# Reading v in long runs, streaming heads in blocks of 64 queries, and half an expert's weights moved

## Chip, cores and metric

One core of one Trainium2 chip. The metric is the device time of one execution in microseconds (us). Most executions agree within 1%; some fall into a slower state (over 1.5% above the fastest of the same kernel), and only fast executions are compared here. A ratio is the mean time of one kernel's fast runs over the mean of the fast runs of the kernel before in the same rounds, on the same chip, so it is not quite the ratio of the medians that I quote. Profiled spans are about 1.5 us shorter than the time of the same execution, and one execution of each kernel was profiled, which need not be its median.

## The reference

Causal attention over 4 batches of 8 heads with 768 positions of 64 numbers. Three heads are retrieval heads (they see everything before), five are streaming heads (they see the first 4 positions, the sinks, and the last 64). The result, 3072 rows of 512, goes through a top-1 mixture of 8 experts with a skip gate.

```python
stream_keep = causal & (is_sink | in_win)          # n_sink 4, window 64
mask = where(is_retrieval, causal, stream_keep)    # heads 1 0 1 0 0 0 1 0
a = softmax(where(mask, scale * q @ k.T, -1e9))
x = (a @ v).transpose(0, 2, 1, 3).reshape(3072, 512)
do = (x @ w_skip) > 0
e = argmax(x @ w_gate)                             # for rows with do
x[do] += softmax(x @ w_gate)[e] * (relu(x @ w1[e]) @ w2[e])
```

## The kernel before

Attention walks over 16 pairs of heads. In each batch three pairs are mixed (retrieval and streaming), one has two streaming heads. In turn i the engines score pair i, transpose q and k of pair i+1, weigh v of pair i-1 and feed the routing of pair i-2. PE, DVE and GpSimd run in the written order.

```python
vv = v.rearrange("b h (n p) d -> b p h n d", p=P)      # 256-byte runs

def cast_v(i):                                          # GpSimd
    va, vx = vab[i % 2], vxb[i % 2]
    nc.gpsimd.tensor_copy(va[:, :, :, :D], v32[i])
    if i:
        nc.scalar.activation(xgs[i], xgs[0], ACT.Copy)
    for hi, hh in enumerate(heads(i)[1]):
        if not IS_RETR[hh]:                             # rows for the window + sinks
            nc.gpsimd.tensor_copy(vx[:, hi], va[:, hi, :NQB - 1])
            nc.gpsimd.tensor_copy(vx[:N_SINK, hi], ...)

# score(i, hi, c0): a streaming head has 11 blocks of 128x128 columns, scored and
# exponentiated in two pieces, 1024 and 384 wide                        (cut)
# weigh(i, hi): streaming heads add va and vx, block by block           (cut)

        ins = nc.gpsimd.tensor_copy(x16s[i], xh[:, :, h2:h2 + 2])
        if i in (0, 5, 10, 11, 12, 13):                 # six halves of weights
            load_weight()
# ... and one more half behind the last gate transpose                  (cut)

for i in range(NPR + 2):
    cast_v(i); load_qk(i + 3); load_v(i + 2)            # bounds cut
    step(0); transpose(i + 1, "q"); step(1); weigh(i - 1, 0)
    step(2); transpose(i + 1, "k"); cast_qk(i + 2)
    # routing of an earlier batch, step(3), gate transpose              (cut)
    weigh(i - 1, 1); step(4)
    # more routing, gate_logits                                         (cut)

gather(0, 4); load_weight(1); gather(4, 6); load_weight(1)
gather(6, 8); load_weight(); rows(0); first(0); rows(1)  # experts follow
```

The softmax here doesn't subtract the row's maximum and nothing guards it: scores larger than these inputs give would overflow.

Of the kernel before, what the change touches and what calls it, by code (L numbers as in the profile page):

```python
# [18 lines left out]
B = 4  # L19
# [240 lines left out]
def kernel(  # L260
# [100 lines left out]
    for e in range(E // 2):  # L361
        for half in range(2):
            wtile(e, half, wpool)
    wtile(E // 2, 0, wpool)
    xgs = [const.tile([P, DM], FP32, name=f"xg{t}") for t in range(NT)]
# [28 lines left out]
    kv = k.rearrange("b h (p n) d -> b p h (n d)", p=P)  # L394
    vv = v.rearrange("b h (n p) d -> b p h n d", p=P)
    Ov = out.rearrange("(b n p) d -> b p n d", b=B, p=P)
# [9 lines left out]
    RLEN = pos  # L406
    SLEN = (2 * NQB - 1) * P
    CH = 1024

    with tc.tile_pool(name="ac", bufs=1) as ac_pool, \  # L410
# [4 lines left out]
         tc.tile_pool(name="st_ps", bufs=2, space=bass.MemoryType.PSUM) as st_psum, \  # L415
         tc.tile_pool(name="tr_ps", bufs=2, space=bass.MemoryType.PSUM) as tr_psum, \
         tc.tile_pool(name="at", bufs=2) as at_pool, \
         tc.tile_pool(name="ov_ps", bufs=2, space=bass.MemoryType.PSUM) as ov_psum, \
         tc.tile_pool(name="oo", bufs=3) as o_pool, \
# [18 lines left out]
        nc.vector.memset(xgs[0], 0.0)  # L438

        NPR = B * H // 2  # L440
        qk32, v32, qk16, qT, ats, xhs, x16s, xTs = ({} for _ in range(8))
        gpss = {}

        def make_masks():





            def select(m, base, column, row):  # L450
                nc.gpsimd.affine_select(
                    out=m, in_=m, compare_op=ALU.is_ge, fill=-MASKED,
                    base=base, pattern=[[column, P]], channel_multiplier=row)

            rmask = ac_pool.tile([P, P], FP16, name="rmask")
            nc.gpsimd.memset(rmask, 0.0)
            select(rmask, 0, 1, -1)
            band = ac_pool.tile([P, P], FP16, name="band")
            nc.gpsimd.memset(band, 0.0)
            select(band, 0, 1, -1)  # L460
            select(band, WINDOW - 1, -1, 1)
            saux = ac_pool.tile([P, P], FP16, name="saux")
            nc.gpsimd.memset(saux, 0.0)
            select(saux, WINDOW - 1 - P, -1, 1)
            nc.gpsimd.memset(saux[:N_SINK], 0.0)
            smask = ac_pool.tile([P, 2 * NQB - 1, P], FP16, name="smask")
            nc.vector.tensor_copy(
                smask[:, :NQB], band.unsqueeze(1).to_broadcast([P, NQB, P]))
            nc.vector.tensor_copy(smask[:N_SINK, 0], rmask[:N_SINK])
            nc.vector.tensor_copy(  # L470
                smask[:, NQB:], saux.unsqueeze(1).to_broadcast([P, NQB - 1, P]))
            return smask.rearrange("p n c -> p (n c)"), rmask

# [14 lines left out]
        def load_v(i):  # L488
            b, hs = heads(i)
            vf = ld_pool.tile([P, 2, NQB, D], FP32, tag="vf", name="vf")  # L490
            for hi, hh in enumerate(hs):
                nc.sync.dma_start(out=vf[:, hi], in_=vv[b, :, hh])
            v32[i] = vf
# [8 lines left out]

        def cast_v(i):
            va, vx = vab[i % 2], vxb[i % 2]
            nc.gpsimd.tensor_copy(va[:, :, :, :D], v32[i])  # L505
            if i:
                nc.scalar.activation(xgs[i], xgs[0], ACT.Copy)  # L507
            for hi, hh in enumerate(heads(i)[1]):
                if not IS_RETR[hh]:
                    nc.gpsimd.tensor_copy(vx[:, hi], va[:, hi, :NQB - 1])  # L510
                    nc.gpsimd.tensor_copy(
                        vx[:N_SINK, hi], va[:N_SINK, hi, 0:1].to_broadcast(
                            [N_SINK, NQB - 1, D + 1]))

# [23 lines left out]

        def pieces(retr):


            work = [(i * P, i, i, 1) for i in range(NQB)]
            if retr:
                for j in range(NQB - 1):
                    work.append((RCOL[j, j + 1], j, j + 1, NQB - 1 - j))
            else:
                for i in range(1, NQB):
                    work.append(((NQB - 1 + i) * P, i - 1, i, 1))
            cut = []
            for (c, j, i, n) in work:  # L550
                while n:
                    m = min(n, 4 - (c // P) % 4)
                    cut.append((c, j, i, m))
                    c, i, n = c + m * P, i + m, n - m
            return cut
# [13 lines left out]
        def score(i, hi, c0):  # L569
            retr = IS_RETR[heads(i)[1][hi]]  # L570
            cn = min(CH, (RLEN if retr else SLEN) - c0)
            pst = st_psum.tile([P, CH], FP32, tag="pst", name="pst")
            mn = S if retr else SLEN
            work = [w for w in pieces(retr) if c0 <= w[0] < c0 + CH]
            for bank in range(c0, c0 + cn, 512):
                mw = min(mn - bank, 512)
                if mw > 0:
                    nc.tensor.matmul(  # L578
                        pst[:, bank - c0:bank - c0 + mw], C.ident,
                        rmask.unsqueeze(1).to_broadcast([P, mw // P, P])  # L580
                        if retr else smask[:, bank:bank + mw],
                        start=True, stop=False)
                here = [w for w in work if bank <= w[0] < bank + 512]
                for (c, j, qb, n) in here:
                    last = (c, j, qb, n) == here[-1]
                    kz, cols = kzb[i % 2][:, hi], slice(c - c0, c - c0 + n * P)
                    if retr or j == qb:
                        nc.tensor.matmul(  # L588
                            pst[:, cols], kz[:, j * P:(j + 1) * P],
                            qT[i][:, qb * P:(qb + n) * P], start=mw <= 0,  # L590
                            stop=mw <= 0 or last)
                        continue


                    nc.tensor.matmul(  # L595
                        pst[WINDOW:, cols], kz[:, j * P + WINDOW:(j + 1) * P],
                        qT[i][:, qb * P:(qb + 1) * P], start=False, stop=last)
                    if last:
                        n0 = sum(w[1] != w[2] for w in here)
                        nc.tensor.matmul(  # L600
                            pst[:WINDOW, c - c0 - (n0 - 1) * P:c - c0 + P],
                            kz[:, :WINDOW],
                            qT[i][:, (qb + 1 - n0) * P:(qb + 1) * P],
                            start=False, stop=True)
            b0 = base(i, hi) + c0
            nc.scalar.activation(ats[i][:, b0:b0 + cn], pst[:, :cn], ACT.Exp,  # L606
                                 scale=SCALE)

        def weigh(i, hi):
# [6 lines left out]
            else:  # L616
                plan = []
                for qb in range(NQB):
                    plan.append((qb, qb * P, va[:, hi, qb]))
                    if qb:  # L620
                        plan.append((qb, (NQB - 1 + qb) * P,
                                     vx[:, hi, qb - 1]))
            opsa = ov_psum.tile([P, NQB, D + 1], FP32, tag="opsa",
                                name="opsa")
            for n, (qb, c, vb) in enumerate(plan):
                nc.tensor.matmul(  # L626
                    opsa[:, qb, :], ats[i][:, b0 + c:b0 + c + P], vb,
                    start=(n == 0), stop=(n == len(plan) - 1))
            if i % 2 == 0 and hi == 0:
# [18 lines left out]
            if not last:  # L648
                ins = nc.gpsimd.tensor_copy(x16s[i], xh[:, :, h2:h2 + 2])  # L649
                if i in (0, 5, 10, 11, 12, 13):  # L650
                    with tc.issue_after(ins.ins):
                        load_weight()
# [11 lines left out]
        def gate_transpose(i):  # L664
# [18 lines left out]
            if i == NPR - 1:  # L683

                nc.gpsimd.tensor_copy(mark, xTg[:, 0, :1])
                load_weight()

        def gate_logits(i):
# [139 lines left out]
        with tc.manual_schedule(engines=engines):  # L828
# [10 lines left out]
            transpose(0, "k")  # L839
            cast_qk(1)  # L840
            for i in range(NPR + 2):
                cur = chunks(i) if i < NPR else []
# [38 lines left out]
                if i > 5 and b < B - 1 and late == 2:  # L881
                    right(b)
                if i >= 2:
                    gate_logits(i - 2)
# [3 lines left out]
            cnt = sums[:, 512:512 + E]  # L888
            idle = st_psum.tile([P, CH], FP32, tag="pst", name="idle")[:, :512]
            place(B - 1)  # L890
            left(B - 1)
# [21 lines left out]
    with tc.tile_pool(name="moe_w", bufs=1) as mw_pool, \  # L913
# [5 lines left out]

        for e in range(E // 2, E):  # L920
            for half in range(2):
# [91 lines left out]
        with tc.manual_schedule(engines={mybir.EngineType.Pool,  # L1013
                                         mybir.EngineType.PE,
                                         mybir.EngineType.DVE}):
            gather(0, 4)
            load_weight(1)
# [64 lines left out]
```

## Time and profile before

| what | where it is read | value |
|---|---|---|
| time | median of 3 executions | 204.39 us |
| span profiled | page | 201.9 us |
| second qT copy (end of the start) | timeline of ACT | 12.5 us |
| second to last qT copy (the loop) | timeline of ACT | 87.3 us |
| last qT copy to first gather (the tail) | timelines of ACT and GpSimd | 27.3 us |
| first gather to the first row cast | timelines of GpSimd and DVE | 3.3 us |
| first gather to the end (routing done, experts) | as above | 74.8 us |

In the profiles PE is TensorE, ACT ScalarE, DVE VectorE and POOL GpSimd; pst are scores in PSUM, at their exponentials, va is v in float16, vx its shifted copy, opsa the weighted sums, xh these sums divided, and qT and kz the transposed q and k. R1 and R2 in the prediction are the two pieces in which a retrieval head is scored.

ACT copies qT out of PSUM exactly once per pair, so these copies are the clock of the loop: their distances are the lengths of the turns.

### The profile page before, as it was taken

How to read it: one execution, taken by the hardware profiler on the slowest of the kernel's cores; microseconds unless marked ns; L12 is line 12 of the kernel's file. 1: busy time of each engine (PE TensorE's matmuls, PEld its weight loads, DVE VectorE, ACT ScalarE, POOL GpSimd, SP SyncE). 2: the span in 40 equal slices, each digit the busy share in tenths (PEclk: the TensorE clock that was granted, in tenths of full speed). 3: DMA queues.
4: the chain of work that ended last, by engine and by line, in shares of the span. 5: the costliest groups of instructions: out<-in, count | busy, mean ns of one | idle time of the engine just before them, and what ended most of it. 6: DMA issues, size and time to landing. Idle time of an engine off the chain costs nothing.

```text
span 201.9 us, 4741 instructions
## 1 busy us (share of the span) xinstructions
PE 163.2 (81%) x1896; PEld 119.3 (59%) x1896; DVE 109.5 (54%) x254; ACT 113.0 (56%) x164; POOL 119.3 (59%) x179
## 2 busy tenths in 40 slices
PE   0487999889888898888982757978999999999920
PEld 0366666676666676666852443378678678665700
DVE  5323666636899668997650678253444534534020
ACT  5998888897688977888891420035143144130400
POOL 7585499687387693788403901687858575133311
PEclk9999999999999999999998795999999999999985
DMA  5999699999899999999999899479999999999501
GB/s 173 295 345 287 169 174 238 316 327 318 236 245 201 301 343 296 342 266 214 215 275 232 204 234 174 103 181 246 232 239 233 239 245 233 235 245 248 165 14 63
DMA packets 47856, 47.12 MB, mean 233 GB/s; under 512 B 28484, under 2 KB 43588, under 8 KB 46802
## 3 DMA queue, kind: packets, MB, share of 16 engines
q0 software_dynamic: 6976, 21.56, 50.3%
q1 hardware_dynamic: 40850, 25.17, 44.3%
q8 instruction: 17, 0.28, 0.6%
q14 instruction: 13, 0.11, 0.2%
HBM read 56.64 MB, written 10.49 MB: 333 GB/s over the span
## 4 chain that ended last, share of the span: by engine, by line
ACT 27%; DMA 26%; PE 23%; issue 8%; DVE 7%; POOL 6%; POOLq 1%; SPq 0%; ACTq 0%; DVEq 0%
ACT at L606 15%; DMA out_dram<-xg,idx_s 14%; DMA vf<-in_v_dram 10%; PE pst L578 5%; ACT xg L507 4%; PE pst L588 4%; PE hps L971 4%; ACT qT L526 4%; ACT gxT L675 3%; PE opsa L626 3%; POOL out_dram L1001 2%; PE pst L595 2%; PE yps L991 2%; POOL xg L935 2%; DMA xg<-out_dram,idx_s 1%
## 5 line engine op out<-in xcount | busy, mean ns | idle before, releaser
L606 ACT ACTIVATE at<-pst 128x1024 f16<-128x1024 f32 (+2 forms) x76 | 61.3, 836 | 17.2 <-PE pst L600 13.3
L978 ACT ACTIVATE ht<-hps 128x512 f16<-128x512 f32 x32 | 19.1, 598 | 49.4 <-PE hps L971 49.4
L588 PE MATMUL pst<-qT,kz 128*128 128x128 f16 (+2 forms) x288 | 35.8, 242 | 2.5 <-ACT qT L526 2.1
L588 PEld LDWEIGHTS <-kz 128*128 128x128 f16 x288 | 24.1, 100 | 21.9 <-issue 12.8
L535 DVE COPY kz<-tps 64x768 f16<-64x768 f16 x28 | 26.6, 950 | 9.7 <-PE tps L518 9.3
L971 PE MATMUL hps<-xT,w 128*128 128x256 f16 x256 | 29.2, 273 | 1.2 <-DVE xT L961 1.2
L971 PEld LDWEIGHTS <-w 128*128 128x128 f16 x256 | 27.9, 113 | 2.8 <-issue 1.5
L578 PE MATMUL pst<-smask,ident 128*128 128x512 f16 (+1 forms) x60 | 22.3, 372 | 8.7 <-ACT at L606 8.7
L991 PE MATMUL yps<-w,ht 128*128 128x512 f16 x128 | 28.8, 379 | 0.0
L1001 POOL DMA_INDIRECT out_dram<-xg,idx_s x16 | 16.4, 1022 | 18.5 <-issue 8.5
L649 POOL CAST gx<-xh 128x768 f16<-128x768 f32 x15 | 12.4, 828 | 19.3 <-DVE xh L641 14.5
L999 DVE SCALAR_TENSOR_TENSOR xg<-yps,gsl,xg 128x512 f32<-128x512 f32 x16 | 12.0, 750 | 20.4 <-PE yps L991 20.3
L626 PE MATMUL opsa<-va,at 128*128 128x65 f16 x372 | 19.8, 196 | 4.0 <-POOL va L505 4.0
L935 POOL DMA_INDIRECT xg<-out_dram,idx_s x16 | 16.8, 1047 | 8.6 <-issue 4.3
L626 PEld LDWEIGHTS <-at 128*128 128x128 f16 x472 | 17.9, 99 | 5.4 <-issue 4.2
L505 POOL CAST va<-vf 128x768 f16<-128x768 f32 x16 | 14.0, 876 | 11.2 <-DMA vf<-in_v_dram 11.1
L637 DVE RECIPROCAL rec<-opsa 128x6 f32<-128x6 f32 x32 | 6.2, 194 | 26.3 <-PE opsa L626 25.9
L991 PEld LDWEIGHTS <-ht 128*128 128x128 f16 x128 | 12.3, 98 | 13.5
L641 DVE TENSOR_TENSOR xh<-opsa,rec 128x384 f32<-128x384 f32 x32 | 17.8, 556 | 1.3
L499 POOL CAST qin<-qf 128x768 f16<-128x768 f32 x16 | 13.1, 818 | 3.3 <-DMA qf<-in_q_dram 3.3
L499 POOL CAST kin<-kf 128x768 f16<-128x768 f32 x16 | 13.1, 822 | 1.0 <-DMA kf<-in_k_dram 0.8
L518 PE MATMUL tps<-ident,qin 128*128 128x128 f16 x96 | 8.7, 231 | 5.9 <-POOL qin L499 5.9
(117 smaller groups left out, 260.7 us busy)
## 6 DMA issues: line engine op xcount, KB each, us to landing
w<-in_moe_w_dram POOLq DMA_DIRECT2D x14, 1024.0 KB, 10.7
qf<-in_q_dram SPq DMA_DIRECT2D x16, 384.0 KB, 6.3
kf<-in_k_dram SPq DMA_DIRECT2D x16, 384.0 KB, 6.0
vf<-in_v_dram SPq DMA_DIRECT2D x32, 192.0 KB, 6.0
out_dram<-xh SPq DMA_DIRECT2D x7, 768.0 KB, 6.8
w<-in_moe_w_dram POOLq DMA_DIRECT2D x4, 512.0 KB, 12.4
out_dram<-xh SPq DMA_DIRECT2D x2, 384.0 KB, 5.2
xg<-out_dram,idx_s POOLq DMA_INDIRECT x16, 7.2
```

What stands on the lines that cost most here:

```text
L499: nc.gpsimd.tensor_copy(h16, qk32[name, i].rearrange("p h n d -> p n h d"))
L535: nc.vector.tensor_copy(to, ti[r])
L578: nc.tensor.matmul(pst[:, bank - c0:bank - c0 + mw], C.ident, rmask.unsqueeze(1).to_broadcast([P, mw // P, P]) if retr else smask[:, bank: ...
L588: nc.tensor.matmul(pst[:, cols], kz[:, j * P:(j + 1) * P], qT[i][:, qb * P:(qb + n) * P], start=mw <= 0, stop=mw <= 0 or last)
L606: nc.scalar.activation(ats[i][:, b0:b0 + cn], pst[:, :cn], ACT.Exp, scale=SCALE)
L626: nc.tensor.matmul(opsa[:, qb, :], ats[i][:, b0 + c:b0 + c + P], vb, start=(n == 0), stop=(n == len(plan) - 1))
L641: nc.vector.tensor_mul(xhs[i // 2][:, :, 2 * (i % 2) + hi, :], opsa[:, :, :D], rec.to_broadcast([P, NQB, D]))
L935: ins = nc.gpsimd.indirect_dma_start(out=xgs[t], out_offset=None, in_=out[:, :], in_offset=bass.IndirectOffsetOnAxis(ap=idx_s[:, t:t + 1], ...
L971: nc.tensor.matmul(hps[:, fi, :], wts[e, 0][:, s].rearrange("p (t c r) -> p t r c", c=P, r=WR)[:, fs // WR, fs % WR], xTs[e][:, s, :], sta ...
L978: nc.scalar.activation(ht[:, 2 * f2:2 * f2 + 2], hps, ACT.Relu)
L991: nc.tensor.matmul(ypss[s2], hts[e][:, fs, s2 * P:(s2 + 1) * P], wts[e, 1][:, fs, :], start=(fs == 0), stop=(fs == FS - 1))
L1001: ins = nc.gpsimd.indirect_dma_start(out=out[:, :], out_offset=bass.IndirectOffsetOnAxis(ap=idx_s[:, t:t + 1], axis=0), in_=xgs[t], in_off ...
```

## The change

Its intent: fewer, longer DMA packets for v; one exponential per streaming head; fewer wasted columns in streaming scores (blocks of 64 queries against 128 keys, sinks of four blocks packed on 32 partitions each); and one half of the weights fewer while attention loads.

```diff
-    vv = v.rearrange("b h (n p) d -> b p h n d", p=P)
+    vv = v.rearrange("b h (m p n) d -> b p h m (n d)", p=P, n=2)   # 512-byte runs
...
+        vsk = ac_pool.tile([P, B * H, 4, D + 1], FP16, name="vsk")
+        nc.vector.memset(vsk, 0.0)
+        def sink_values():                       # once, behind cast_qk(1)
+            for g in range(4):
+                nc.gpsimd.dma_start(out=vsk[32 * g:32 * g + N_SINK, :, g, :D],
+                                    in_=v.rearrange("b h s d -> s (b h) d")[:N_SINK])
...
         def cast_v(i):
-            nc.gpsimd.tensor_copy(va[:, :, :, :D], v32[i])
+            nc.gpsimd.tensor_copy(v16[i]..., v32[i])
+        def order_v(i):                          # at the end of turn i
+            for half in range(2):
+                vps = tr_psum.tile(...)
+                for n in range(2):
+                    nc.tensor.matmul(vps, pick[:, half, n], v16[i][:, :, :, n], ...)
+                to = va[:, :, half::2, :D]
+                if half == 0: nc.scalar.activation(to, vps, ACT.Copy)
+                else:         nc.vector.tensor_copy(to, vps)
+            shift_v(i)                           # GpSimd makes vx out of va
...
+        def score_near(i, hi, pst):              # two masks, 1 + 5 + 10 + 5 matmuls
+            ...                                  # then one exponential of 1024
...
-                if i in (0, 5, 10, 11, 12, 13):
+                if i in (0, 5, 10, 12, 13):
                     load_weight()
...                                              # behind the last gate transpose
                 load_weight()
+                load_weight(1)
...
-            gather(0, 4)
+            gather(0, 2)
+            load_weight(1)
+            gather(2, 4)
             load_weight(1)
```

The weighted sums get one PSUM buffer instead of two, the transposes three instead of two. `load_weight()` moves one half of an expert's weights, `load_weight(1)` half of that: so the half that leaves the attention goes in two parts, one at the attention's end and one between the first gathers. Cut from the diff are ones written into the sink table, and the copies that clear the experts' row buffers (xg): they are written at other places, but in both profiles all 15 still run on ACT before 16 us, outside the loop.

## The prediction

> **What bounds the kernel now.** I read the page first, then stretches of time, the waits, the chain of waits, and last the timelines of PE and DVE. There are two stages: attention (16 pairs of heads) up to about 120 us, then routing and the experts from 127 us, where PE is busy without a gap from 144 to 192 us. The change is in the first stage. On the page, the DMA row and the row of the queue that carries q, k, v and the stores:
> ```profile
> DMA  5999699999899999999999899479999999999501
> ...
> q1 hardware_dynamic: 40850, 25.17, 44.3%
> ```
> The DMA engines are at 90% in nearly every slice. Of 40850 packets 24576 are v's (32 heads x 768 rows of 256 bytes). What those cost shows in two stretches (columns: PE, PEld, DVE, ACT, POOL busy, PE clock, DMA share, GB/s), the first with q and k alone (1536-byte runs), the second with v:
> ```profile
> 7.00:8.00 1.00, 0.62 (x3) 0.03 (x1) 0.77 (x1) 1.00 (x3) 0.00 (x0) 1.00 1.04 372
> 9.50:10.00 0.50, 0.33 (x4) 0.33 (x4) 0.00 (x0) 0.50 (x2) 0.20 (x2) 1.00 1.40 232
> ```
> So a pair of heads needs three 393 KB moves (q, k, store) at 372 GB/s = 3.2 us and v at 232 = 1.7 us: 4.9 us. Sixteen pairs are 78 us. A half of an expert's weights (2 MB read) takes about 5.7 us, from four of them beside the loads of 87 to 111 us; six halves are 34 us. With 2.5 us of start that is 115 us of DMA for a stage of 120. Where it gives way, the waits tell:
> ```profile
> POOL va L505 <- DMA vf<-in_v_dram: 11.1, 2, 10.1
> ...
> PE opsa L626 <- POOL va L505: 4.0, 1, 4.0
> ```
> One v load, caught between four halves of weights in a row, held GpSimd for 10.1 us and PE for 4.0. Everywhere else attention walks at its own pace, a (retrieval, streaming) pair per 6.05 us. The chain of waits over one such pair:
> ```profile
> 57.16 0.38 PE pst L578
> ...
> 58.36 1.02 ACT at L606
> 59.38 0.70 ACT gxT L675
> 60.09 0.39 ACT at L606
> 60.48 0.04 issue
> 60.52 1.02 ACT at L606
> 61.54 0.70 ACT qT L526
> 62.25 0.93 ACT at L606
> 63.17 0.04 issue
> 63.21 0.38 PE pst L578
> ```
> Read it as a loop: PE scores the first streaming piece (1.20 us to ACT's start); ACT does its exponential, gxT, the 384-wide exponential, then R1, qT, R2 of the next pair; only when R2 is read does the score buffer come free for the next streaming piece. PE's side of the same loop is as long:
> ```profile
> 57.16 0.38 PE L578 MATMUL pst<-smask,ident 128*128 128x512 f16 x1 [0.85 <-ACT at L606]
> ...
> 58.25 0.51 PE L667 MATMUL xtp<-ident,gx 128*128 128x128 f16 x6
> 58.60 0.23 PE L626 MATMUL opsa<-va,at 128*128 128x65 f16 x2
> ...
> 58.93 0.33 PE L578 MATMUL pst<-smask,ident 128*128 128x384 f16 x1
> ...
> 59.48 0.39 PE L578 MATMUL pst<-rmask,ident 128*128 128x512 f16 x1
> ```
> Score 1.09, gate transpose 0.35, weigh 0.33, second streaming piece 0.55, then R1 0.78 (to 60.26): 3.10 us, and ACT starts R1 at 60.52, only 0.26 later. Last, DVE at the start:
> ```profile
> 1.18 1.87 DVE L429 MEMSET kz<- 64x384 uint32 x4 [1.18 <-PEq L1063]
> 3.10 0.48 DVE L438 MEMSET xg<- 128x512 f32 x1
> ...
> 7.23 1.94 DVE L535 COPY kz<-tps 64x768 f16<-64x768 f16 x2 [2.50 <-PE tps L518]
> ```
> DVE is free at 4.7 and waits for the first transposes; the copies of k then open the scores, and the first exponential starts at 11.6.
>
> **What the Trainium skill says.** "DMA: Bandwidth & Descriptors", Specifications, asks for at least 512 bytes for line rate, with a read-modify-write below; the 232 against 372 GB/s above agrees. "TensorEngine Tiling (Array Packing)", Key Properties, says that changing the tiling mode drains TensorE. The trace agrees: the last 128-column score starts at 57.87 and streams 0.05, and the first 64-column one starts at 58.02, 0.10 us lost; the same on the way back. "TensorE: Matmul & The Clock Gate", Back-to-back issue gap, gives N/2.4 + 2.5 ns; the 512-wide mask matmul occupies 0.22 us (57.16 to 57.37), which agrees. "VectorE: DVE Perf Modes", Zero memsets can be issued as uint32, says that a memset takes one cycle per element whatever the type; here 384 elements took 378 ns and 512 took 485.
>
> **The change, part by part.**
> v in 512-byte runs: at 340 to 370 GB/s a pair's v takes 1.1 us instead of 1.7, 16 x 0.6 = 9 us of DMA. One half fewer in attention: 5.7 us. DMA need falls from 115 to about 100 us, so the v wait goes. Worth: PE's 4.0 us and about 1 us of half clock behind it, -5 us. This is the only gain on the path that I am sure of.
>
> v put in order on chip: per pair four matmuls of 384 columns (4 x 0.16 = 0.64 us of PE), a 384-wide copy on ACT (about 0.40 net, as the 384-wide exponential) and one on DVE (0.5, beside other work).
>
> One exponential per streaming head: 20 x 0.49 us of ACT go, but 16 x 0.49 come back as the v copy. In the loop above the 0.39 piece is simply replaced by a 0.40 copy: nothing gained on ACT.
>
> Streaming scores: two masks 0.44, one 128x128 and five 64-wide matmuls 0.21, a drain 0.10, ten 64x64 on two column tiles side by side (5 x 0.055 = 0.28), a drain 0.10, five sinks on four 32-column tiles 0.13, a drain 0.10: 1.36 us, against 1.09 + 0.55. Streaming weigh: six 128-wide at 0.03 = 0.18, two drains 0.20, ten half-width 0.28: 0.66 against 0.33.
>
> PE's loop becomes 1.36 + 0.35 + 0.66 + 0.64 + 0.78 = 3.79, +0.69. ACT's becomes 1.45 (PE, with the latency) + 4.85 = 6.30, because the streaming piece now comes as one block, +0.25. So a mixed pair goes from 6.05 to between 6.3 and 6.75; I take +0.5. Eleven such pairs lie between the first and the last steady pair: +5.5 us. Pairs of two streaming heads have fewer waits for ACT: about -0.4 each, -1 us in all.
>
> The start: in the changed program DVE clears a table of sink values, 8320 float16 per partition in one memset, ahead of the masks and ahead of the first k copies. At about 1 ns per element that is 8.0 to 8.7 us, from 3.9 to about 12.4. Behind it stand four copies for the picking matrix, some ten small memsets and three mask copies, about 2.7 us. The first k copy starts near 15.2 instead of 7.23, the first score near 16.4 on a half-speed PE, the first exponential near 17.5 instead of 11.6: +6 us, and DMA, stopped by full load buffers, idles. GpSimd's four small sink transfers wait for the same memset, about 4 us of issue before v's first cast, near 18: in time.
>
> Fewer PSUM buffers for the weighted sums (two to one): the second weigh of a pair waits for DVE's division, about 1 us after the first. In mixed pairs the weighs are 3 us apart: free. In double streaming pairs 0.7: a few tenths, counted in the -0.4.
>
> Experts: attention leaves five halves loaded and issues one and a half more at its end, against six and one. DMA stood half idle from 128 to 135 us and has about 5 us of slack at the last weights, so 5.7 us more fit: 0 to +1.
>
> Sum: -5 + 6 + 5.5 - 1 + 0.5 = +6, about 210. I shade it to 208.5: the loop's +0.5 stands on narrow matmuls of which this trace shows few, and a step in a line of tuning is seldom kept for being slower.
>
> **The rivals.**
> (a) DMA was the true bound of attention all along: 115 of 120 us speak for it. Then 15 us of DMA relief show as a faster stage, and if the memset overlaps better than I think, 197 to 201. Against it: the 6.05 us loop is closed by PE and ACT without any DMA wait, and only one wait of 10 us breaks it.
> (b) PE becomes the bound: column tiles that do not run side by side, or more drains, give +1.2 us per mixed pair and 213 to 217. For it: the PE loop was already within 0.26 us of ACT's. Against it: at 58.02 two tiles start together.
> (c) The start and the wait cancel and the loop grows by only 0.2: 203 to 206, a large change that moves little.
> (d) The half moved past attention meets the gathers, and the experts wait for weights: +3 us more. Slack of 5 us speaks against it.
>
> **Range and chances.** The start (+6) and the removed wait (-5) are each good to 2 us, the loop (+2 to +9) is the wide term, the experts 0 to 3. Hence 201 to 216. Faster by over 2% (below 200.3) needs the memset off the path or the loop shorter: 0.17. Within 2%: 0.33. Slower: 0.50.
>
> **What would show it.** In the changed profile: DVE's memset of the sink table 8 to 9 us long, and the first exponential at 17 to 18 us (start). The wait of GpSimd for v gone from the waits view, and rates near 350 GB/s while v loads (DMA). R1 to R1 of a mixed pair at 6.3 to 6.8 us, with 0.10 us gaps before narrow matmuls, and ACT waiting for PE's streaming scores about 0.9 us a pair (loop). Experts still without a PE gap, at the same length from first gather to end (experts). I am wrong if the first exponential stays near 12 us, if the loop stays at 6.05 or falls, or if a new wait on the single sum buffer or on the shifted v appears with over 2 us in total.

## More of the kernel before

The lines that bear on the limit stand in the prediction. One more, of the page, the chain that ended last by engine:

```profile
ACT 27%; DMA 26%; PE 23%; issue 8%; DVE 7%; POOL 6%; POOLq 1%; SPq 0%; ACTq 0%; DVEq 0%
```

DVE has 7% of the chain.

## The result, and the profile after

The changed kernel took 218.63 us (median of 4, 218.18 to 219.95) against 204.88 us of the kernel before in the same rounds: ratio 1.070, 95% interval 1.062 to 1.078. It is slower, by more than the top of my range.

The queue that carries q, k, v and the stores did what was intended, 12288 packets fewer:

```profile
DMA  5979599999569989747996994999999999999811
...
q1 hardware_dynamic: 28562, 25.17, 38.1%
```

But the DMA row now has holes, and the queue's work only fell from 44.3% of 201.9 us to 38.1% of 216.6, which is 89.4 to 82.5 us: 7 us. The chain that ended last has changed hands, DVE from 7 to 27%:

```profile
DVE 27%; PE 19%; DMA 17%; ACT 12%; issue 11%; POOL 11%; POOLq 1%; ACTq 0%; DVEq 0%
```

The start, in DVE's timeline (columns: start, busy, engine, line, operation, tiles, sizes):

```profile
5.55 6.99 DVE L453 MEMSET vsk<- 128x8320 f16 x1 [1.68 <-issue]
...
15.56 1.87 DVE L592 COPY kz<-tps 64x768 f16<-64x768 f16 x2
```

The clear of the sink table stands ahead of the first copy of k, which starts at 15.56 instead of 7.23. The first exponential comes at 17.78 instead of 11.60.

The loop, in PE's waits (columns: who waited for what, us in total, times, longest):

```profile
PE opsa L708 <- POOL vx L570: 8.2, 4, 2.8
...
PE opsa L703 <- DVE va L558: 2.5, 2, 1.8
```

These are new: the weighing waits for v, whose ordered rows come from DVE and whose shifted copy comes from GpSimd. One of these places in full, first in the chain that ended last, then in the timeline:

```profile
71.05 1.17 DVE Rall L903
72.21 0.12 DVE ohn L908
...
72.36 0.04 DVE acc L909
...
72.44 0.57 DVE va L558
...
73.05 0.76 PE opsa L703 x19
```

```profile
72.44 0.56 DVE L558 CAST va<-vps 128x384 f16<-128x384 f32 x1
73.05 0.76 PE L703 MATMUL opsa<-va,at 128*128 128x65 f16 x19 [1.76 <-DVE va L558]
73.13 0.45 POOL L569 COPY vx<-va 64x325 f16<-64x325 f16 x1 [1.33 <-DVE va L558]
```

DVE's copy of v out of PSUM is written at the end of a turn, so it stands in DVE's queue behind that turn's routing work (Rall, ohn, acc). PE waits 1.76 us for it and GpSimd 1.33, and only then can GpSimd make the shifted copy.

The spans laid side by side, each number from the timelines as in the table above:

| stretch, us | before | after | difference | predicted |
|---|---|---|---|---|
| start, to the second qT | 12.5 | 18.7 | +6.2 | +6 |
| loop, second to last qT | 87.3 | 97.6 | +10.3 | +5.5 - 1 |
| tail, last qT to first gather | 27.3 | 25.1 | -2.2 | -5 |
| first gather to the end | 74.8 | 75.2 | +0.4 | +0.5 |
| span | 201.9 | 216.6 | +14.7 | +6 |

So 5.8 us of the excess are in the loop and 2.8 in the tail. The loop's growth is uneven. Three of its turns, those from the ninth to the eleventh and from the thirteenth to the fourteenth qT, hold 6.1 us of it (1.6, 1.5 and 3.0); between undisturbed mixed pairs a turn takes 6.51 us where it took 6.05.

### The profile page after: what moved, and what is told of

Read it like the earlier page. It is cut to its first block, busy times and chain, and to the rows that moved or that the text cites. A ratio compares the mean times of both kernels' runs of the same rounds, so it can differ in the third digit from the quotient of the medians.

```text
span 216.6 us, 5477 instructions
## 1 busy us (share of the span) xinstructions
PE 171.0 (79%) x2200; PEld 126.2 (58%) x2200; DVE 126.6 (58%) x287; ACT 112.8 (52%) x160; POOL 122.5 (57%) x184
## 3 DMA queue, kind: packets, MB, share of 16 engines
q1 hardware_dynamic: 28562, 25.17, 38.1%
## 4 chain that ended last, share of the span: by engine, by line
DVE 27%; PE 19%; DMA 17%; ACT 12%; issue 11%; POOL 11%; POOLq 1%; ACTq 0%; DVEq 0%
DMA out_dram<-xg,idx_s 13%; ACT at L650 6%; DVE kz L592 5%; POOL xg L1024 4%; DMA xg<-out_dram,idx_s 4%; DVE vsk L453 3%; DVE xh L724 3%; POOL out_dram L1090 3%; PE pst L657 3%; PE vps L551 2%; PE pst L644 2%; ACT qT L583 2%; PE opsa L703 2%; ACT at L629 2%; DVE Rall L903 2%
## 5 line engine op out<-in xcount | busy, mean ns | idle before, releaser
L650 ACT ACTIVATE at<-pst 128x1024 f16<-128x1024 f32 (+1 forms) x36 | 32.2, 922 | 14.8 <-PE pst L644 14.7
L644 PE MATMUL pst<-qT,kz 128*128 128x128 f16 (+2 forms) x168 | 22.4, 258 | 8.9 <-DVE kz L592 8.9
L629 ACT ACTIVATE at<-pst 128x1024 f16<-128x1024 f32 x20 | 20.5, 1025 | 10.7 <-PE pst L675 10.4
L720 DVE RECIPROCAL rec<-opsa 128x6 f32<-128x6 f32 x31 | 6.1, 196 | 28.2 <-PE opsa L708 14.7
L644 PEld LDWEIGHTS <-kz 128*128 128x128 f16 x168 | 13.7, 102 | 13.1 <-DVE kz L592 9.5
L703 PEld LDWEIGHTS <-at 128*128 128x128 f16 x372 | 14.7, 98 | 6.4 <-issue 3.3
L703 PE MATMUL opsa<-va,at 128*128 128x65 f16 x271 | 14.0, 193 | 2.5 <-DVE va L558 2.5
L657 PE MATMUL pst<-smask,ident 128*128 128x512 f16 x40 | 12.3, 391 | 4.5 <-ACT at L650 4.4
L551 PE MATMUL vps<-vin,pick 128*128 128x384 f16 x64 | 13.6, 327 | 1.8 <-ACT va L556 1.3
L758 ACT ACTIVATE gxT<-xtp 128x768 f16<-128x768 f16 x15 | 12.1, 807 | 5.3 <-PE xtp L750 5.3
L1040 DVE CAST x<-xg 128x512 f16<-128x512 f32 x16 | 9.7, 637 | 8.5 <-DMA xg<-out_dram,idx_s 8.5
```

The source lines that it names most:

```text
L629: nc.scalar.activation(ats[i][:, b0:b0 + SLEN], pst, ACT.Exp, scale=SCALE)
L644: nc.tensor.matmul(pst[:, c - c0:c - c0 + n * P], kzb[i % 2][:, hi, j * P:(j + 1) * P], qT[i][:, qb * P:(qb + n) * P], start=mw <= 0, stop ...
L650: nc.scalar.activation(ats[i][:, b0:b0 + cn], pst[:, :cn], ACT.Exp, scale=SCALE)
L657: nc.tensor.matmul(pst[:, bank * 512:(bank + 1) * 512], C.ident, smask[:, bank * 512:(bank + 1) * 512], start=True, stop=False)
L703: nc.tensor.matmul(opsa[:, qb, :], ats[i][:, b0 + c:b0 + c + P], vb, start=(n == 0), stop=(n == len(plan) - 1 and not near))
```

## The experiments

The theories: **O**, the ordering of v on chip costs far more than its work, through its place in the queues; **S**, the start costs what was predicted; **G**, the moved half of weights costs by meeting the gathers; **B**, nothing of this, the blocks of 64 are what is slow. The texts on record split O in two: V, v's new path over PE, DVE and GpSimd arrives late, and P, its work lengthens PE's own loop. Their D is DMA as the bound.

### 1. The clear later and halved, the sink transfers later

```diff
-        nc.vector.memset(vsk, 0.0)                # at once
-            sink_values()                         # before the first turn
+            # clear as uint32 (4160 words), after the first copies of k
+            # sink_values() in turn 0, after cast_qk(2)
```

> The changed kernel, with the table of sink values cleared as uint32 and only after the first two copies of k, and the four small sink transfers issued behind the first cast of v. Theory S (the memset ahead of the first k copy delays the whole pipeline): the first exponential comes at 11 to 12.5 us instead of 17.8, and the time falls by 5 to 6 us, to about 213. Rival (DMA or a later wait would absorb it): the first exponential moves but the time falls by under 2 us.

217.28 us (216.17 to 218.11), ratio 1.064: only about 1 us, as the rival had it. The clear took 3.52 us and the second qT came at 11.99, as hoped. But the turn from the third to the fourth took 11.5 us. Three stretches (columns: busy time of PE, PEld, DVE, ACT, POOL with counts, PE clock, DMA share, GB/s):

```profile
12.00:18.00 6.00, 5.08 (x73) 3.71 (x73) 4.36 (x8) 6.00 (x10) 5.03 (x7) 1.00 1.04 303
18.00:24.00 6.00, 2.91 (x47) 1.97 (x43) 1.61 (x3) 3.66 (x5) 2.82 (x4) 0.90 0.98 119
24.00:30.00 6.00, 6.00 (x64) 3.66 (x62) 2.94 (x17) 2.22 (x3) 4.34 (x7) 0.54 0.68 150
```

From 18 to 24 us the DMA engines are busy (0.98) but move only 119 GB/s: the four sink transfers, 16 KB each onto 4 partitions, are issued between 14.5 and 17.5, and PE's three waits for them end between 22.5 and 23.9. PE then runs at about half clock (0.54). The kernel of experiment 6 without these transfers (203.9 us) moves 262 GB/s from 18 to 24 us. So the start has two costs, and in the changed kernel one hid behind the other: there PE never waits for the sink transfers. Moving both is no test of S; experiments 4 and 6 separate them.

### 2. The same ordering at two other places of the turn

```diff
-                if i < NPR: order_v(i)            # at the turn's end
+                if i < NPR: order_v(i)            # late: after step(3); early: before it
```

> The changed kernel, with the v ordering matmuls right behind the streaming scores, ahead of the gate transpose and of the second weigh. PE does the same work between the streaming scores and R1, so PE's loop is as long as before the edit; but DVE's copy of v and GpSimd's shift no longer queue behind the weigh, its division and the routing. Theory V (v's new path over PE, DVE and GpSimd arrives late): the waits of the weigh for v's copies and shifts (10.7 us in total) nearly vanish and the time falls by 4 to 7 us, to 212 to 215. Theory P (PE's loop of 0.45 us more per pair is the cost): no change, within 1 us.

> The changed kernel, with the v ordering matmuls ahead of the streaming scores, where PE waits for ACT anyway. Theory V: as e2, 4 to 7 us less. Theory P: a mixed pair falls from 6.5 to about 5.8 us, because the 0.66 us leaves the loop from the streaming scores to R1, and the time falls by 6 to 8 us. Both: 10 to 13 us less, to 206 to 209.

Late: 217.1 us, ratio 1.064; early: 216.65, ratio 1.061. In the early profile the loop falls from 97.6 to 94.2 us and the first gather comes 5.1 us sooner; between undisturbed mixed pairs the turn is 5.86. But more than half of it is given back: the first row is cast 6.8 us after the first gather instead of 5.2, probably because the weights issued just ahead have had less time to land, and gather to end grows from 75.2 to 78.0. Both runs miss their forecasts (212 to 215, and 206 to 209). The signs of V and P did appear in the early run: the mixed turn is 5.86, and PE no longer waits for v's copies. But GpSimd now waits 20.5 us for them in 13 places, and PE waits elsewhere, for a cast of v on GpSimd (1.3 us at 65.7) and for a copy of k on DVE (2.2 us at 103.0). So the place in the queues matters, as O says, but it is not all.

### 3. v in 256-byte runs again, the rest as changed

```diff
-    vv = v.rearrange("b h (m p n) d -> b p h m (n d)", p=P, n=2)
+    vv = v.rearrange("b h (n p) d -> b p h n d", p=P)
-            nc.gpsimd.tensor_copy(v16[i]..., v32[i])
+            nc.gpsimd.tensor_copy(va[:, :, :, :D], v32[i]); shift_v(i)
-                if i < NPR: order_v(i)
```

> The changed kernel, with v loaded in runs of 256 bytes and cast straight into place as before; no ordering matmuls and no copies of them. Theory D (DMA was the bound, and the 512-byte runs earn their cost): the time is the same or longer than 218.6, with a v wait of 5 us or more back. Theories V and P: the loop falls to about 5.8 us, no waits for v's path, and the time falls by 6 to 12 us in spite of 9 us more of DMA, to 207 to 212.

206.8 us, ratio 1.009 (0.994 to 1.023): 12 us come back, as V and P forecast (6 to 12). The loop is 86.9 us, the tail 22.4. B falls, and so does D: without the ordering, the blocks of 64 and the rest of the change leave the loop where it was (87.3), with the 6.2 us of start still in. And the wait for v's transfer that the long runs were to remove stays away without them: GpSimd waits for it 2.2 us at most.

The turns of the changed kernel minus those of this one sum to 10.7 us, and five turns of the fourteen hold 9.0 of it: 1.6 and 1.5 in the turns behind those of double-streaming pairs, 1.5, 1.5 and 2.8 in the next ones, beside the routing of an earlier batch. PE's waits for v's copies in the changed kernel sum to 7.9 us up to the last qT and 2.8 behind it; this run has none of them. (They do not simply add up to the cost: this run waits 6.7 us for DVE's division, the changed kernel 1.4.)

### 4. v in long runs alone, on the kernel before

```diff
 # kernel before, plus only: vv in 512-byte runs, v16, pick, order_v at the turn's end
```

> The kernel before with one part of the change alone: v read in 512-byte runs, cast to a staging tile and ordered on chip by four matmuls with a 0/1 matrix, one ScalarE and one VectorE copy per pair, at the same place in the loop. Theory V (ordering v in line costs 0.5 to 0.8 us per pair and more around the routing, against which the DMA saves little): 211 to 217 us, the qT intervals sum to 8 to 12 us more than before, partly paid back by 2 us at the end of the attention where the wait for the v transfer goes. Rival (the ordering only costs together with the streaming blocks, whose shifted v is made from it by GpSimd): 204 to 207 us.

221.79 us (221.17 to 222.76), ratio 1.086: more than the whole change. The loop is 107.3 us. A mixed turn takes 7.02 us instead of 6.05, that of a double-streaming pair 10.67 instead of 7.35. With experiment 3 this shows in both directions that **the ordering of v is the costly part**; how much of that is its place in the queues is shown by the waits and, in part, by experiment 2. It is dearer here than in the changed kernel. One reason stands in this trace, in each of the two turns of 10.67 (here the first):

```profile
52.74 2.60 DVE L756 TENSOR_TENSOR sub<-glog,mx 128x48 f32<-128x48 f32 x1
```

A subtraction of the routing, 0.21 us at its shortest in the kernel before, takes 2.60 us here and ends 0.06 us after the last of four GpSimd instructions in a row (the same sign as in experiment 7); over its three calls in the loop that is 5.6 us too much. In the changed kernel such delays do not tell the kernels apart: over DVE's instructions up to 142 us, what they take above the shortest of their kind (where it is over 0.15 us) sums to 8.2 us, against 8.0 in the kernel before and 9.7 in experiment 3. ACT's second exponential per streaming head, still there beside the new copy of 0.50 us, may cost too; that was not tested.

### 5. The weight loads: six halves again, five halves alone

```diff
-                if i in (0, 5, 10, 12, 13):       # and load_weight(1) at the end
+                if i in (0, 5, 10, 11, 12, 13):   # on the changed kernel, and on that of experiment 6
```

> The changed kernel with only the order of the weight loads put back to six halves in the attention. If the moved half costs by meeting the gathers: the first row is cast 3.5 us after the first gather instead of 5.2, total 217 us (-1 to -2). If the change needed the room (rival: DMA limits these pairs): same or slower, 218 to 220.

> The same with the order of the weight loads put back to that of the kernel before (six halves in the attention, one at its end, all of the first four gathers ahead of the next). Theory (the half that was moved to the end of the attention meets the first gathered rows on the DMA engines): first gather to first cast of a row back from 5.9 to about 3.5 us, gather to end 75 us instead of 77.6, total 1.5 to 3 us below the run without this edit, so 198 to 200. Rival (the sixth half slows the loads of q, k and v by as much as it saves later): the same time within 1 us, with the intervals of qT from the eleventh to the fourteenth pair 1 to 2 us longer in sum.

On the changed kernel it makes no difference (218.31 us, ratio 1.068): the first row is cast 3.4 us after the first gather instead of 5.2, as G says, but from gather to end it is 76.1 us instead of 75.2. On the kernel with short runs and a mended start (203.9, next experiment) it makes 213.92 where 198 to 200 was expected, and its fastest run is 208.57. The profile (of a slow run, so its size is not used) shows the wait that the change was to remove, for the last v:

```profile
POOL va L530 <- DMA vf<-in_v_dram: 10.9, 1, 10.9
PE opsa L699 <- POOL vs L561: 9.5, 1, 9.5
```

Then the reverse, the third part of the change alone on the kernel before:

```diff
-                if i in (0, 5, 10, 11, 12, 13):   # kernel before
+                if i in (0, 5, 10, 12, 13):       # + load_weight(1) at the end, gathers split
```

> The kernel before with only the order of the weight loads of the change: five halves in the attention, one and a half at its end. Theory (the fourth half in a row holds the last v back): the wait of GpSimd for v falls from 10.1 us to under 5, last qT to first gather 22.5 to 25 us instead of 27.3, against 1 to 2 us that the first rows wait longer behind the gathers: 201 to 204 us. Rival (the moved half costs what it saves): 204 to 206.

**201.71 us (200.86 to 202.22), ratio 0.986 (0.983 to 0.989)**: this is the best of all the kernels, for the smallest edit. The 10.1 us wait of GpSimd for v is gone:

```profile
POOL va L505 <- DMA vf<-in_v_dram: 2.6, 2, 1.6
```

The tail is 22.4 us instead of 27.3: the predicted 5 us. Against that, the loop is 88.3 us instead of 87.3, the first row is cast 5.5 us after the first gather instead of 3.3, and gather to end is 76.0 instead of 74.8. So G is seen, as a small charge on a larger gain. Long runs and five halves are two cures for one wait. Five halves alone are enough; with long runs and six halves it is gone as well (2.2 us at most on the changed kernel), but those loops are 10 to 20 us longer, which gives the transfers more time, so that long runs alone cure it is not shown. The change pays for both, and the expensive one was not needed.

### 6. The start: sink rows made on chip, or the clear alone

Short runs leave v in place, so each pair can copy its four sink rows out of its own v into a tile for two heads, with no table and no transfers.

```diff
-        vsk = ac_pool.tile([P, B * H, 4, D + 1], FP16)      # clear, 4 transfers
+        vsb = [tile([P, 2, 4, D + 1]) for _ in range(2)]    # cleared once, 0.49 us each
+        for g in range(4):                                  # per pair, on GpSimd
+            nc.gpsimd.tensor_copy(vs[32 * g:32 * g + N_SINK, h, g], va[:N_SINK, h, 0])
```

> The kernel with v in 256-byte runs (206.8 us, 1.009 of the kernel before), and in it the start mended: the 128x8320 clear (6.99 us of DVE) and the four sink transfers are gone; each pair copies its sink rows from its v on chip with four small GpSimd copies into a tile of two heads. Theory S (the clear and the sink transfers together cost the start 6 us, one hiding behind the other, which is why moving both gave only 1 us in the earlier run): 200 to 202 us, first exponential near 11.6 us, and the step from the second to the third qT copy back to about 6 us. Rival (the start would be bound by the first loads or by the masks anyway): 204 to 207 us. If the extra GpSimd copies delay the shifted v, the interval of double-stream pairs grows by 0.5 us or more.

203.91 us, ratio 0.999 (0.992 to 1.006). The second qT comes at 11.98 instead of 18.71, so S holds: 6.7 us. But the loop is now 3.4 us longer and the tail 2.9, so the total misses the 200 to 202 expected; GpSimd has 64 more copies of 250 ns and is busy 138.7 us instead of 125.7.

The clear put back by itself, on the kernel of experiment 7 (218.2 us):

```diff
+        nc.vector.memset(vsk, 0.0)                # 128x8320, no sink transfers
```

> The kernel of the first run of this group with the 128x8320 clear put back at its old place, but without the sink transfers. Theory S (the clear by itself holds the start, 6.99 us on VectorE ahead of the first k copies): the second qT copy at 18 to 18.7 us instead of 12, total 5 to 6.5 us above the first run of this group. Rival (the sink transfers were the larger part, the clear overlaps the first loads): under 2 us above it.

227.14 us; by the ratios of fast runs, 1.103 against 1.067, about 7 us more. (The profile is of a slow run; its second qT, at 19.9 us, is not used.) S again, and a little more than expected: **the clear by itself holds the start**. In the changed kernel the sink transfers, which cost nearly as much when they were exposed in experiment 1 (its loop is 5.7 us longer), hid behind it.

### 7. Why small copies on DVE are so dear

To give GpSimd its time back I put the four copies on DVE, at the end of the turn.

```diff
-                nc.gpsimd.tensor_copy(vs[...], va[:N_SINK, h, 0])
+                nc.vector.tensor_copy(vs[...], va[:N_SINK, h, 0])
```

> The kernel with v in 256-byte runs and sink rows copied on chip (203.9 us), with the four copies of each pair on VectorE at the end of the pair's turn instead of on GpSimd at its start. Theory (the loop's return of 3.4 us from the second to the last qT copy, 86.9 to 90.3, and of 3 us behind the last one is GpSimd's: 64 small copies of 250 ns stand ahead of the casts of q and k): qT from the second to the last copy 87 us again, total 199 to 201 us, faster than the kernel before by 2 to 3%. Rival (the faster start only moves the loop against the DMA rate, which gives the time back anyway): 203 to 204 us, with new DMA waits in the loop.

218.21 us, ratio 1.067. A miss of 18 us, which taught the most. The loop grew from 90.3 to 102.8. Two sum buffers do not help:

```diff
-         tr_ps bufs=3, ov_ps bufs=1
+         tr_ps bufs=2, ov_ps bufs=2
```

> The same with two buffers for the weighted sums and two for the transposes, as in the kernel before (the change has one and three). If the single sum buffer costs (the waits of the weigh for the division were 6.7 us in sum in the run of 256-byte runs): 1 to 3 us below the run beside it. If these waits lie beside others: within 0.5 us, or slower by up to 2 us as the transposes of q, k, the gate and the routing then share two buffers.

219.93 us, ratio 1.073: no gain. As this kernel is held up elsewhere, it is a weak test of the single sum buffer.

Was DVE's queue too full, or was something holding it? The same work, made as a reduction over one element:

```diff
-                nc.vector.tensor_copy(vs[...], va[:N_SINK, h, 0])
+                nc.vector.tensor_reduce(vs[...], va[:N_SINK, h, 0].unsqueeze(3),
+                                        axis=AX.X, op=ALU.add)
```

> The kernel with the sink copies on VectorE (218.2 us), each made by a reduction over an axis of one element instead of a copy: same engine, same place, same data. Theory L (a VectorE copy from SBUF to SBUF in float16 waits until GpSimd's running instruction ends, and holds GpSimd in turn; the Trainium skill, SBUF - State Buffer, says a reduction never does): each takes 150 to 200 ns instead of a median of 423, qT from the second to the last copy 86 to 89 us instead of 102.8, total 199 to 203 us. Rival Q (VectorE's in-order queue is simply full, 64 more instructions are too many): 212 to 217 us, in proportion to the busy time.

205.44 us, ratio 1.008, above the 199 to 203 expected: but 12 to 13 us from the choice of instruction. The two lines of the tile vs, copies first (columns: minimum, median and maximum in ns):

```profile
L567 DVE COPY vs<-va x64: 164/423/1475, 15.5 to 128.3; 4x65 f16<-4x65 f16 x48, 4x130 f16<-4x130 f16 x16
```

```profile
L568 DVE TENSOR_REDUCE vs<-va x64: 200/214/282, 15.4 to 114.1; 4x65 f16<-4x65 f16 x48, 4x130 f16<-4x130 f16 x16
```

A copy takes 164 ns or up to 1475, a reduction 200 to 282. The Trainium skill, "SBUF — State Buffer", Who interferes with whom, says that DVE and GpSimd share one pair of ports under an exclusive lock, that copies can take it, that the loser waits for the whole instruction, and that a reduction never does. The runs agree: same engine, same place, same data, and only the form of the instruction differs. The trace of the copies shows the wait itself: 29 of the 64 take 164 to 191 ns, and of the 35 longer ones 34 end 29 to 55 ns after a GpSimd instruction ends. Four copies in a row, with GpSimd beside them:

```profile
42.56 1.97 DVE L567 COPY vs<-va 4x65 f16<-4x65 f16 x4
42.71 0.83 POOL L730 CAST gx<-xh 128x768 f16<-128x768 f32 x1 [1.57 <-DVE xh L722]
43.48 0.83 POOL L530 CAST va<-vf 128x768 f16<-128x768 f32 x1
```

The first and the last of the four take 0.17 and 0.18 us, the two between them 0.83 and 0.77, until gx and then va are cast. Theory L (the lock) holds, and its rival, a full queue, falls: the reductions leave as many instructions in DVE's queue. Some cost remains, as the loop is 89.8 us and the tail 24.2, against 86.9 and 22.4 with the table in their place.

The same copies on ACT, and on GpSimd at the end of the turn:

```diff
-                nc.vector.tensor_copy(vs[...], va[:N_SINK, h, 0])
+                nc.scalar.activation(vs[...], va[:N_SINK, h, 0], ACT.Copy)   # e14
+                nc.gpsimd.tensor_copy(vs[...], va[:N_SINK, h, 0])            # e15
```

> The same four copies on ScalarE. [...]about 0.2 us each, 0.8 us a pair, of which 0.39 is what the single exponential freed. Theory L and Q both take VectorE out of it: 200 to 206 us. If ScalarE closes the loop of a mixed pair: intervals of 6.3 to 6.8 us and 204 to 209.

> The same four copies on GpSimd, at the end of the turn instead of at its start as in the run of 203.9 us. If what that run gave back in the loop (3.4 us) was the casts of q and k standing behind the copies: 200 to 202 us. If it is GpSimd's total (16 us more of work) or the lock against VectorE: 203 to 206.

ACT: 207.83 us, ratio 1.018 (profiled in a slow run, so not read further), above the range of the theory and inside that of its alternative. GpSimd late: 212.35, ratio 1.042, a miss: I had thought that the copies only stood in the way of the casts of q and k at the turn's start (203.9). At its end they come too late, and PE waits 9.2 us for them in 8 waits.

### 8. Three attempts to go further

Both copies of the ordering on ACT, on the changed kernel with the early ordering:

```diff
-                if half == 0: nc.scalar.activation(to, vps, ACT.Copy)
-                else:         nc.vector.tensor_copy(to, vps)
+                nc.scalar.activation(to, vps, ACT.Copy)
```

> The changed kernel with the ordering of v ahead of the streaming scores (216.65 us when run so) and both of its copies out of PSUM on ScalarE, none on VectorE. Theory (VectorE's queue is what ends the waits around the routing: k copies, division, routing operations): 16 x 0.56 us leave VectorE, qT from the second to the last 94.2 -> 90 to 92 us, total 213 to 215. Rival (ScalarE is as full, its queue closes the loop of a mixed pair): the same or slower, 216 to 221.

215.52 us, ratio 1.054 against 1.061: 1 us at best, within the error; the loop is 95.4 us instead of the 90 to 92 expected. The turns where DVE routes shorten by 0.3 to 0.7 us, those of double-streaming pairs lengthen by up to 1.0. Inconclusive.

The half of weights behind the gathers, and the reductions ahead of the routing:

```diff
-                load_weight(1)                     # e16: at attention's end
-            gather(0, 2); load_weight(1); gather(2, 4)
+            gather(0, 4)                           # e16: both parts of the half
+                                                   # come behind gather(4, 6)
-                if i < NPR: sink_rows(i)           # e17: at the turn's end
+                # e17: after cast_qk(i + 2)
```

> The kernel of the first run of this group, and the half of weights that the change issues at the attention's end is issued only after the first six gathers. Theory (it meets the gathered rows on the DMA engines): the first row is cast 3.3 to 4 us after the first gather instead of 5 to 7, total 1 to 2.5 us below the first run of this group. Rival (these loads are needed that early; the last experts wait for their weights): same or slower by 1 to 3 us, with PE waiting for weights.

> The kernel with v in 256-byte runs and the sink rows made by reductions on VectorE (205.4 us), with these placed after the k copies of the turn and ahead of its routing work, instead of at the end of the turn. If the last loss is that TensorE waits for them behind the routing work (7.4 us in 3 waits, intervals of 8.1 us at two places where the run without them has 6.1): these waits gone, qT from the second to the last copy 86 to 88 us instead of 89.8, total 201 to 204. Rival (the intervals are set by VectorE's sum of work): 204 to 206, the wait only moves.

e16: 209.05 us, ratio 1.030. The rows did come 4.0 us after the gather instead of 5.2, but PE then waited 2.7 us for weights, as the rival said. The first gather came 3.3 us later, which this edit should not touch; but the execution profiled took 212.03 us, 3 us more than four of the other five, and that of e13 was its fastest (203.48), so this may be one run against another. e17: 205.57, ratio 1.005, as without it. The wait only moved, as the rival said; PE now waits for the division:

```profile
PE opsa L703 <- DVE xh L724: 11.2, 10, 2.3
```

## Why the prediction was wrong

The direction and most of the mechanisms were right; the size was not. By the steps of the prediction:

1. **The start, +6.** Right: +6.2, and the clear alone makes 7 us. That the number fits is partly luck, as two errors cancel: the clear took 6.99 us and not 8.0 to 8.7, but 1.7 us ahead of it, in which DVE waited for nothing that the profile shows, filled the gap.
2. **The v wait, -5.** Right as a mechanism: five halves alone bring 4.9 us of tail, and so do they with the blocks of 64 (22.4 us in both). In the changed kernel only 2.2 is seen, as the last pair's v has to be ordered before it is weighed: 25.1 against 22.4, so 2.7 goes to point 4.
3. **Streaming scores, one exponential, narrow matmuls.** Right in detail, and harmless: where I read it undisturbed, the score block took 1.22 us (1.36 estimated), the weighing 0.56 (0.66). The narrow tiles do run two at a time (pairs of 64-column matmuls start 4 ns apart), so rival (b) falls. In a kernel without the ordering the loop is 86.9 us against 87.3.
4. **The failed step: "v put in order on chip".** The prediction put it at 0.64 us of PE and 0.40 of ACT a pair, with DVE's copy "beside other work", and all parts together at +0.5 for eleven mixed turns. In undisturbed mixed turns that is what is seen (6.05 to 6.51). What failed is "beside other work". The copy is a link of a chain, PE, ACT and DVE, then GpSimd's shifted copy, then PE's weighing; it stands in DVE's in-order queue behind the routing and in GpSimd's behind the casts. Taking the ordering out gives 10.7 us in the loop and 2.7 in the tail, less 2.4 which the gathers then lose: 11 us; for the loop, with all parts, I had 4.5. Adding it to the kernel before costs about 17.5. PE's waits for v's copies are 7.9 us in the loop and 2.8 behind it, so the path is seen in the trace. The test of the place alone (experiment 2) is weaker: moving the ordering ahead of the routing took 3.4 us off the loop, and the other 7.3 stayed. Which queue holds those is not shown; taking DVE out of the path (experiment 8) did not free them.
5. **Double-streaming pairs, -0.4 each.** Wrong sign: +0.3 to +0.5 in the turn of such a pair, and the turn behind it is 1.5 us longer than without the ordering. Of waits, I looked at the sum buffer, but PE waits for the shifted v, 8.2 us in four places. I had written that such a wait over 2 us would prove me wrong, but gave it no part of the range.
6. **Experts, +0.5.** Right in sum (+0.4). Rival (d), the moved half meeting the gathers, is real: with five halves the first row comes 1 to 4 us later behind the gather than the 3.3 us of six. Where five halves were tried alone, that made 1.2 us from gather to end; on the changed kernel six halves instead of five gained nothing there.
7. **Rival (a), DMA as the true bound.** It falls: with v in 256-byte runs again the loop is as short as before (86.9 us), and one half of weights less in the kernel before leaves it at 88.3, while in the changed kernel holes opened in the DMA row. Rival (c) falls by the result.

Last, I shaded the sum from 210 to 208.5 because a step in a line of tuning is seldom kept for being slower. No line of a profile stood behind that.

What stays open: why the ordering costs an undisturbed mixed turn of the kernel before more than one of the changed kernel (0.97 against 0.65, which is 6.51 less the 5.86 of experiment 3) is argued from ACT's load, not tested. And the blocks of 64, with the five halves and the best start I found, end at 203.9, above the five halves alone; where the rest of their gain goes is not settled.

## What to carry to other kernels

When a change buys DMA time with work on engines, ask which engine's queue the result of that work must pass before the next engine can go on; a copy of half a microsecond that is free by busy time can cost several times that where it stands behind a burst of other work (here three turns grew by 1.5 to 3.0 us each). If a change has several parts that cure the same wait, run each alone: here the cheapest one gave all the gain. And where DVE and GpSimd both copy within SBUF, the form of the instruction (reduction or copy) can matter more than its size (here 12 to 13 us).

## What the Trainium skill lacked or had wrong

- "VectorE: DVE Perf Modes", Zero memsets can be issued as uint32, says one cycle per element. From that and 384 elements in 378 ns I estimated 8.0 to 8.7 us for 8320 float16 elements; it took 6.99 us. All five sizes cleared in these runs (384, 512, 520, 4160 and 8320 elements in 378, 485, 492, 3525 and 6992 ns) fit 58 ns plus 0.833 ns an element, whether float16, float32 or uint32, so that the type does not matter agrees. The page names no fixed part; I had spread it over the elements of the short ones.
- "TensorEngine Tiling (Array Packing)", Key Properties, says that a change of mode drains TensorE but gives no time. The traces show 0.10 us each way.
- "SBUF — State Buffer", Who interferes with whom, is right about the lock, but does not show how much it takes from a kernel in which both engines copy all the time: 64 copies onto 4 partitions, of 65 to 130 elements, took 164 to 1475 ns each and 12 to 13 us of the whole; as reductions 200 to 282 ns.
- I found no page that says what small transfers onto 4 partitions do to the loads beside them: with four of 16 KB under way the DMA engines stood at a share of 0.98 for 6 us with 119 GB/s moved (experiment 1; 262 GB/s in the same stretch without them), and in the changed kernel they landed about 7 us after their issue.
